# Windowed attention and a gated MLP on one core: softmax sums of four heads in one step, products in 32-column strips, layer norm on three engines, and a new order of all steps

## The chip, the core and the metric

The kernel runs on one core of a Trainium2 chip. The core has a tensor engine (PE; its weight loads are listed apart as PEld), a vector engine (DVE), a scalar engine (ACT), a general engine (POOL) and a sync engine (SP), which issues nearly all DMAs here. Each engine works through its own list of instructions in order, and semaphores hold an instruction back until what it needs is there. Matrix products write to PSUM, of which the kernel uses eight banks of 128 partitions by 512 floats. The metric is the time of one execution on the device in microseconds; lower is better.

## What is computed

Eight batches of eight heads, 576 positions, 64 values per head. First attention over a causal window of 64 positions, then a gated MLP over each position's 512 values, with a layer norm and a product along the positions in it:

```python
scores = scale * np.matmul(q, k.transpose(0, 1, 3, 2))
mask = (rel >= 0) & (rel < window)                 # window = 64
attn = softmax(np.where(mask, scores, -1e9))
x = np.matmul(attn, v)                             # heads side by side: (8, 576, 512)
h = np.maximum(x @ w_in, 0.0)                      # w_in 512 x 1024
u, v = h[..., :512], h[..., 512:]
v_n = (v - mu) / np.sqrt(var + 1e-06)
v_s = np.einsum('ts,bsd->btd', w_spatial, v_n) + b_spatial[None, :, None]
out = (u * v_s) @ w_out                            # (8, 576, 512), float32
```

## The kernel before

Everything is written as named steps, and a step belongs to one engine. `kernel` builds the steps; the text `ORDER` (lines 18 to 145) lists every one of them with its engine and its buffers or PSUM banks, and the instructions are emitted in just that order. So the order of the work on every engine, that of the loads on SP included, is written out by hand. `BUFS` says how many buffers of each kind there are.

The steps, with b for the batch, g for a group of four heads (0 or 1), u for a pair of heads in it:

- `ldq`, `ldk`, `ldv` load a group's inputs (V in five parts); `cq`, `ck`, `cv` cast them to 16 bits on ACT, POOL or DVE (line 292, 295, 298 or 300 in the profile); `tq`, `tk` transpose q and k on DVE (L419); `sl`, `su`, `s4` make `hs`, a copy of V shifted by 64 positions.
- `S` (L479) computes the scores of a group: for seven chunks of keys, four heads and two halves of the head's values, 56 matmuls with 32 rows each, the four heads in four row strips of the array, into two pairs of banks. `E` (ACT, L486) takes the exponential, `M` (DVE, L489) masks it by a minimum.
- `Z` (L502) sums over keys with a matrix of ones: one step for each pair of heads, two matmuls with 64 weight columns over 512 columns. `N` (L529) and `n` (L531) on ACT turn the sums into their inverses by a logarithm and an exponential. `P` (L514) multiplies with V: 14 matmuls for a pair of heads, 64 weight columns each. `X` (DVE, L522) multiplies the two.
- The names ending in `_r` do the same for the last 64 positions of a batch; for batches 4 and 5, and 6 and 7, two batches share these steps (L553 to L606).
- `V` and `U` multiply x with the two halves of w_in, five steps each for a batch; `Vr` (ACT, L670) and `Ur` (ACT, L764) apply the maximum with zero. `Vb`, `Va` (DVE, L672, L674) take mean and variance, `L1`, `L2` (ACT, L717, L719) make the inverse deviation, and `A` (DVE, L729) normalizes, five steps for a batch.
- `G` multiplies with w_spatial along the positions, `Ge` (DVE, L798, L801) multiplies by u, `O` multiplies with w_out, `Oe` (ACT, L647) copies the result out of PSUM, and `st` stores it.
- `D` are warm-up matmuls on zeros (L844), `W` transposes of w_spatial (L378), `ldwin`, `cwin`, `ldwsp`, `cwsp`, `ldwo`, `cwo`, `We` and so on load and prepare the weights.

`V`, `U`, `G` and `O` steps have four or five matmuls of 128 weight columns over 512 columns. In `ORDER` such a step is marked PE, or PH; with PH, `halves` (line 612) issues each matmul as two of 64 weight columns, in the same strips of the array as `Z` and `P`. The fifth step of each (`U_4`, `G_4`) has the last 64 positions: 16 or 20 matmuls over 64 columns (128 where two batches share `U_4`).

Of the kernel before, what the change touches and what calls it, by code (L numbers as in the profile page):

```python
# [10 lines left out]
AF = mybir.ActivationFunctionType  # L11
ALU = mybir.AluOpType
# [18 lines left out]
sl0_11:DVE su0_11:POOL cwin110:POOL N0_r:ACT:4 cwin111:POOL ck1_1:POOL:2 E1_00:ACT:1 X0_00:DVE:0
cwin101:ACT P0_11:PE:3 ldwin011:DQ ldwsp3:DQ:5 ldwsp2:DQ:7 P0_10:PE:1 X0_01:DVE X0_10:DVE:1 n0_r:ACT
D3:PE:0 cq1_1:POOL:0 X0_11:DVE E1_01:ACT:0 ldwsp1:DQ:6 ldwsp4:DQ:1 ldv1_00:DQ:2 P0_r:PE:2 D19:PE:0
V0_2:PH:1 Vr0_2:ACT:0 M1_00:DVE M1_01:DVE X0_r:DVE:0 ldwsp0:DQ:2 V0_3:PH:0 Vr0_3:ACT:1 tk1_1:DVE:6
cwin000:POOL Z1_00:PE:3 N1_00:ACT:5 ldv1_01:DQ ldv1_02:DQ V0_0:PH:1 Vr0_0:ACT:2 tq1_1:DVE:7
cwin010:DVE Vb0_2:DVE:0 cwin001:POOL Vb0_0:DVE:1 n1_00:ACT V0_4:PE:0 V0_1:PH:2 Vr0_4:ACT:3
Z1_01:PE:3 Vb0_4:DVE:2 N1_01:ACT:1 Vb0_3:DVE:3 S1_1:PE:1:0 cwin011:POOL Va0_4:DVE E1_11:ACT:3
E1_10:ACT:2 Va0_0:DVE M1_11:DVE Vr0_1:ACT:4 Vb0_1:DVE:4 cwsp3:POOL:8 U0_0:PE:1 Ur0_0:ACT:0 U0_4:PH:0
cb:POOL cwsp2:ACT ldv1_03:DQ U0_1:PH:3 Ur0_1:ACT:1 Va0_3:DVE U0_2:PE:2 Va0_1:DVE Va0_2:DVE L10:ACT:0
M1_10:DVE Z1_11:PE:1 S1_r:PE:0:1 Ur0_4:ACT:2 L20:ACT A0_1:DVE:0 ldv1_04:DQ U0_3:PE:3 cwsp1:POOL:0  # L40
cwsp4:DVE A0_4:DVE cwsp0:POOL:1 W1:PE:0 E1_r0:ACT:0 A0_0:DVE:1 E1_r1:ACT M1_r:DVE cv1_00:POOL:2
N1_11:ACT:0 ldk2_0:DQ:3 ldv1_10:DQ:3 Ur0_3:ACT:3 W3:PE:1 ldv1_11:DQ ldq2_0:DQ:4 We1:ACT ldv1_12:DQ
W4:PE:3 ldv1_13:DQ We3:ACT cv1_01:DVE We4:DVE sl1_00:DVE:2 W2:PE:0 ldv1_14:DQ ldk2_1:DQ:5 sl1_01:DVE
Ur0_2:ACT:4 ldwo10:DQ:0 ldq2_1:DQ:6 W0:PE:1 We0:DVE Z1_r:PE:3 su1_00:POOL ldwo00:DQ:7 We2:ACT
su1_01:POOL s41_0:POOL cv1_10:POOL:3 sl1_10:POOL:3 N1_r:ACT:2 A0_3:DVE:2 ldwo11:DQ Z1_10:PE:2
N1_10:ACT:3 A0_2:DVE:3 ldwo01:DQ n1_01:ACT P1_00:PE:0 X1_00:DVE:2 P1_01:PE:1 X1_01:DVE n1_10:ACT
G0_0:PH:3 Ge0_0:DVE:0 ldq3_0:DQ:2 ldv2_00:DQ:0 G0_4:PE:2 G0_3:PE:0 ldk3_0:DQ:1 Ge0_4:DVE:1
ck2_0:ACT:1 tk2_0:DVE:2 su1_10:POOL cq2_0:ACT:3 cv1_11:POOL sl1_11:POOL Ge0_3:DVE:2 G0_2:PE:1
s41_1:ACT tq2_0:DVE:3 su1_11:ACT ldv2_01:DQ ldv2_02:DQ ldv2_03:DQ G0_1:PE:3 P1_10:PE:2 P1_11:PE:0
S2_0:PE:0:1 n1_11:ACT X1_10:DVE:3 X1_11:DVE V1_0:PE:2 Ge0_2:DVE:3 ldv2_10:DQ:1 ldv2_11:DQ ldv2_12:DQ  # L50
ldk3_1:DQ:3 U1_1:PE:0 E2_00:ACT:1 M2_00:DVE Ge0_1:DVE:4 E2_01:ACT:0 M2_01:DVE cwo10:POOL
ck2_1:POOL:2 Ur1_1:ACT:5 V1_1:PE:1 ldv2_13:DQ Vr1_1:ACT:5 tk2_1:DVE:4 ldv2_14:DQ ldv2_04:DQ
Vr1_0:ACT:6 Vb1_0:DVE:5 n1_r:ACT V1_2:PE:3 ldv3_10:DQ:2 ldq3_1:DQ:4 P1_r:PE:0 cq2_1:POOL:0 cwo01:ACT
Vr1_2:ACT:7 U1_2:PE:1 cwo00:POOL X1_r:DVE:1 Vb1_1:DVE:2 Va1_0:DVE Ur1_2:ACT:0 cwo11:POOL ldv3_11:DQ
V1_3:PE:2 Vr1_3:ACT:4 Z2_00:PE:0 tq2_1:DVE:5 Vb1_2:DVE:1 N2_00:ACT:4 Va1_1:DVE Z2_01:PE:3
N2_01:ACT:5 V1_4:PE:1 Vr1_4:ACT:3 cq3_0:POOL:1 Oe0_4:ACT:0 U1_3:PH:2 Va1_2:DVE tq3_0:DVE:6
ck3_0:POOL:3 Vb1_4:DVE:3 Vb1_3:DVE:4 S2_1:PE:0:1 E2_10:ACT:2 M2_10:DVE Va1_3:DVE O0_0:PE:0 Va1_4:DVE
tk3_0:DVE:7 E2_11:ACT:3 M2_11:DVE Oe0_0:ACT:0 O0_1:PE:3 Oe0_1:ACT L11:ACT:1 L21:ACT A1_1:DVE:4
A1_0:DVE:5 A1_3:DVE:6 A1_2:DVE:7 A1_4:DVE Ur1_3:ACT:2 cv2_00:POOL:1 sl2_00:POOL:0 su2_00:POOL
O0_2:PE:1 S2_r:PE:0:1 U1_4:PH:0 E2_r0:ACT:0 E2_r1:ACT M2_r:DVE ldv3_12:DQ ldq4_0:DQ:5 ldv3_13:DQ  # L60
cv2_10:POOL:0 U1_0:PH:3 Ur1_0:ACT:3 Z2_10:PE:2 ldv5_10:DQ:3 S3_0:PE:0:1 Ur1_4:ACT:4 Z2_11:PE:3
Oe0_2:ACT:1 n2_00:ACT n2_01:ACT N2_11:ACT:1 G1_3:PH:0 Ge1_3:DVE:5 s42_0:ACT sl2_10:POOL:1 G1_0:PH:1
Ge1_0:DVE:6 ldv3_00:DQ:0 s42_1:ACT su2_10:POOL Z2_r:PE:0 N2_r:ACT:3 N2_10:ACT:0 ldq4_1:DQ:6
ldk4_0:DQ:7 O0_3:PH:3 Oe0_3:ACT st0_1:DQ P2_00:PE:1 X2_00:DVE:0 G1_4:PH:0 Ge1_4:DVE:7 n2_10:ACT
P2_01:PE:2 X2_01:DVE n2_11:ACT ldv4_00:DQ:1 P2_10:PE:3 X2_10:DVE:1 P2_11:PE:1 n2_r:ACT G1_1:PH:0
X2_11:DVE cq3_1:ACT:2 P2_r:PE:2 X2_r:DVE:0 E3_00:ACT:1 ck3_1:POOL:0 U2_0:PE:3 V2_1:PE:1 Vr2_1:ACT:2
Ur2_0:ACT:1 tq3_1:DVE:0 V2_3:PE:2 ldv3_01:DQ ldv3_02:DQ ldv3_03:DQ ldv3_14:DQ cq4_0:POOL:1
Ge1_1:DVE:8 Vr2_3:ACT:1 tk3_1:DVE:1 tq4_0:DVE:8 V2_0:PE:0 U2_4:PE:1 E3_01:ACT:0 M3_01:DVE
Vr2_0:ACT:0 Vb2_0:DVE:0 Ur2_4:ACT:2 st0_4:DQ ldk4_1:DQ:0 cv3_10:POOL:2 Vb2_1:DVE:5 V2_2:PE:3
Vr2_2:ACT:5 st0_0:DQ ldv3_04:DQ S3_1:PE:0:1 E3_10:ACT:2 E3_11:ACT:3 U2_2:PH:2 Ur2_2:ACT:3 G1_2:PH:0  # L70
Vb2_2:DVE:2 Z3_01:PE:1 Vb2_3:DVE:1 N3_01:ACT:2 M3_11:DVE Va2_0:DVE S3_r:PE:0:1 E3_r0:ACT:0 Va2_3:DVE
E3_r1:ACT V2_4:PE:3 Vr2_4:ACT:6 ck4_0:POOL:3 Z3_11:PE:2 N3_11:ACT:4 Ge1_2:DVE:9 O1_2:PH:1
Oe1_2:ACT:1 U2_1:PH:0 Oe1_4:ACT:0 M3_r:DVE Va2_2:DVE Z3_r:PE:2 N3_r:ACT:5 U2_3:PH:1 Vb2_4:DVE:4
M3_10:DVE Va2_4:DVE cq4_1:POOL:2 Va2_1:DVE O1_3:PH:3 L12:ACT:0 L22:ACT M3_00:DVE Z3_10:PE:2
tq4_1:DVE:2 tk4_0:DVE:3 Ur2_3:ACT:4 Ur2_1:ACT:5 A2_0:DVE:0 A2_1:DVE:1 N3_10:ACT:0 Oe1_3:ACT A2_4:DVE
A2_2:DVE:2 A2_3:DVE:3 sl3_10:POOL:2 su3_10:POOL O1_0:PH:1 Z3_00:PE:0 N3_00:ACT:1 s43_1:POOL
ck4_1:POOL:0 cv3_00:POOL:3 sl3_00:POOL:3 s43_0:POOL O1_1:PH:2 ldv4_10:DQ:2 Oe1_0:ACT:0 P3_11:PE:3
ldq5_1:DQ:2 ldq5_0:DQ:1 st1_4:DQ P3_10:PE:0 cq5_1:POOL:1 n3_10:ACT X3_10:DVE:2 ldv5_00:DQ:0
# [821 lines left out]
```

## Time and profile before

| | us |
|---|---|
| three runs | 197.14, 199.26, 199.71 |
| median | 199.26 |
| span of the profiled execution, first to last instruction | 196.2 |
| PE busy, matmuls | 185.6 |
| DVE busy | 161.2 |
| ACT busy | 154.3 |
| POOL busy | 105.5 |

The profiled execution's whole time is not listed beside its span. Busy time is the time in which an engine has at least one instruction running; as matmuls overlap, a busy PE can still be slower or faster than its best. Starts of PE's instructions are therefore of more use than their lengths: the distance from the first matmul of a step to the first of the next is what the step costs.

### The profile page before, as it was taken

Reading aid. Unit: us, or ns where it says so; the run is one execution under the profiler, and the core shown is the slowest. Engines: PE = TensorE matmul, PEld = TensorE weight load, DVE = VectorE, ACT = ScalarE, POOL = GpSimd, SP = SyncE. Lnnn points to the kernel's source line nnn. Section 1 sums busy time; section 2 is a strip of 40 time slices with the busy share of each in tenths; the row PEclk is TensorE's granted clock in tenths of the full one; section 3 lists DMA queues with packets and bytes.
Section 4 is the critical chain, followed back from the end, with each engine's and each line's share of the span. In section 5 each row is a group of like instructions: output and inputs, shape, how many; then the busy total and the mean of one; then the engine's idle time right before and its main releaser. Section 6 shows DMA issues by size and latency. Waiting matters only on the chain.

```text
span 196.2 us, 7598 instructions
## 1 busy us (share of the span) xinstructions
PE 185.6 (95%) x3211; PEld 105.8 (54%) x3211; DVE 161.2 (82%) x297; ACT 154.3 (79%) x275; POOL 105.5 (54%) x188
## 2 busy tenths in 40 slices
PE   7789899899999999999999998999999999999991
PEld 2334545545454655665565655665765565655550
DVE  4699999999998899999999995979985983846440
ACT  2479779995998989997899996888897997736331
POOL 4265684857988549950999965939756000000000
PEclk9999999999999999999999999999999999999999
DMA  6996999999989988698977799496934002400625
GB/s 207 397 294 172 354 358 252 278 336 381 264 207 283 334 225 242 192 253 240 331 201 233 160 267 327 78 295 197 344 120 147 3 3 109 133 7 0 226 74 189
DMA packets 50277, 42.73 MB, mean 218 GB/s; under 512 B 39361, under 2 KB 39489, under 8 KB 50242
## 3 DMA queue, kind: packets, MB, share of 16 engines
q1 hardware_dynamic: 50018, 41.91, 71.8%
q8 instruction: 25, 0.41, 1.0%
q10 hardware_dynamic: 224, 0.33, 0.5%
q14 instruction: 10, 0.08, 0.2%
HBM read 32.79 MB, written 9.44 MB: 215 GB/s over the span
## 4 chain that ended last, share of the span: by engine, by line
PE 70%; DVE 15%; DMA 6%; ACT 4%; issue 2%; POOL 1%; SPq 0%; DVEq 0%; POOLq 0%
PE bank L617 48%; PE bank L614 7%; PE bank L514 4%; PE pair L479 4%; PE bank L703 3%; DMA out_dram<-ob 3%; DMA nk<-in_k_dram 3%; PE bank L502 2%; DVE kT L419 2%; DVE vn L729 2%; ACT e L486 2%; DVE qT L419 2%; DVE e L489 2%; DVE st L672 1%; DVE hv L300 1%
## 5 line engine op out<-in xcount | busy, mean ns | idle before, releaser
L617 PE MATMUL bank<-wspT,vn 128*64 128x512 f16 (+3 forms) x460 | 35.7, 300 | 0.6 <-DVE vn L729 0.6
L486 ACT ACTIVATE e<-pair 128x1024 f16<-128x1024 f32 x32 | 31.6, 1024 | 5.6 <-PE pair L479 4.8
L295 POOL CAST hk<-nk 128x384 f16<-128x384 f32 x42 | 23.4, 593 | 16.8 <-DMA nk<-in_k_dram 16.5
L647 ACT COPY ob<-bank 128x512 f32<-128x512 f32 (+1 forms) x39 | 22.4, 593 | 10.9 <-PE bank L617 7.7
L617 PE MATMUL bank<-x,win 128*64 128x512 f16 (+2 forms) x368 | 30.2, 304 | 0.0
L798 DVE TENSOR_TENSOR g<-bank,ru 128x512 f16<-128x512 f32 (+1 forms) x36 | 22.9, 650 | 7.2 <-PE bank L617 6.7
L617 PE MATMUL bank<-wout,g 128*64 128x512 f16 x232 | 28.5, 379 | 0.0
L672 DVE BATCH_NORM_STATS2 st<-vs 128x6 f32<-128x512 f16 (+1 forms) x40 | 25.8, 668 | 3.0 <-ACT vs L670 2.8
L670 ACT ACTIVATE vs<-bank 128x512 f16<-128x512 f32 (+1 forms) x40 | 23.2, 598 | 5.9 <-PE bank L617 3.1
L298 POOL COPY hs<-hv 64x512 f16<-64x512 f16 (+1 forms) x44 | 26.3, 624 | 1.2
L764 ACT ACTIVATE ru<-bank 128x512 f32<-128x512 f32 (+1 forms) x38 | 21.8, 581 | 5.8 <-PE bank L617 5.5
L489 DVE TENSOR_TENSOR e<-e,mask 128x1024 f16<-128x1024 f16 x32 | 24.0, 762 | 2.6 <-ACT e L486 2.5
L617 PEld LDWEIGHTS <-vn 128*64 128x64 f16 (+1 forms) x460 | 18.3, 110 | 13.6 <-DVE vn L729 2.0
L617 PE MATMUL bank<-win,x 128*64 128x512 f16 x192 | 24.3, 379 | 0.0
L522 DVE TENSOR_TENSOR x<-bank,lz 128x512 f16<-128x512 f32 x32 | 20.9, 681 | 3.9 <-PE bank L514 3.8
L295 POOL CAST hq<-nq 128x384 f16<-128x384 f32 x33 | 17.3, 560 | 10.4 <-DMA nq<-in_q_dram 10.3
L419 DVE STREAM_TRANSPOSE qT<-hq 128x576 f32<-128x576 f32 x16 | 19.8, 1240 | 2.6 <-ACT hq L292 2.5
L419 DVE STREAM_TRANSPOSE kT<-hk 128x576 f32<-128x576 f32 x16 | 19.7, 1239 | 0.5 <-POOL hk L295 0.5
L617 PEld LDWEIGHTS <-win 128*64 128x64 f16 x368 | 15.1, 111 | 9.3 <-issue 0.8
L529 ACT ACTIVATE lz<-bank 128x512 f32<-128x512 f32 x32 | 19.1, 603 | 0.8 <-PE bank L502 0.8
L531 ACT ACTIVATE lz<-lz 128x512 f32<-128x512 f32 x32 | 19.5, 631 | 0.3
L729 DVE TENSOR_SCALAR vn<-vs,mv,ln 128x512 f16<-128x512 f16 (+1 forms) x40 | 17.7, 492 | 2.3 <-ACT ln L719 2.3
(89 smaller groups left out, 294.1 us busy)
## 6 DMA issues: line engine op xcount, KB each, us to landing
nq<-in_q_dram SPq DMA_DIRECT2D x16, 576.0 KB, 6.6
nk<-in_k_dram SPq DMA_DIRECT2D x16, 576.0 KB, 5.5
nv<-in_v_dram SPq DMA_DIRECT2D x64, 128.0 KB, 5.2
out_dram<-ob SPq DMA_DIRECT2D x14, 512.0 KB, 5.5
wi<-in_moe_w_in_dram SPq DMA_DIRECT2D x8, 256.0 KB, 5.6
ws<-in_moe_w_spatial_dram SPq DMA_DIRECT2D x4, 288.0 KB, 7.3
nv<-in_v_dram SPq DMA_DIRECT2D x16, 64.0 KB, 4.9
wo<-in_moe_w_out_dram SPq DMA_DIRECT2D x4, 256.0 KB, 7.2
```

What stands on the lines that cost most here:

```text
L295: nc.gpsimd.tensor_copy(o[:, n:n + 384], i[:, n:n + 384])
L298: nc.gpsimd.tensor_copy(o[:, lo:hi, :, :], i[:, lo:hi, :, :])
L419: d = add(f"t{name}{b}_{g}", ("DVE", 1.09), key, lambda e: nc.vector.transpose(qt.t[:, :].rearrange("p (i j) -> p j i", j=18), h.t[:, :].b ...
L486: ex = add(f"E{b}_{g}{u}", ("ACT", 0.91), key, lambda e, u=u: nc.scalar.activation(e2[u].t[:, :, :], sc[u].t[:, :, :], AF.Exp, bias=0.0, s ...
L489: mins.append(add(f"M{b}_{g}{u}", ("DVE", 0.65), key, lambda e, u=u: nc.vector.tensor_tensor(e2[u].t[:, :, :], e2[u].t[:, :, :], mask[:, : ...
L617: nc.tensor.matmul(o[c:c + 64, :], w[:, c:c + 64], x, start=start, stop=stop)
L647: lambda e: (nc.vector.tensor_copy if last else nc.scalar.copy)(view(), m.t[rows, 0:n]),
L670: rl = add(f"Vr{b}_{j}", ("ACT", 0.49), key, lambda e: nc.scalar.activation(vs.t[0:jn, :], m.t[0:jn, :], AF.Relu), deps=[pv], acq=[vs], us ...
L672: s1 = add(f"Vb{b}_{j}", ("DVE", 0.6), key + 0.02, lambda e: nc.vector.bn_stats(st6.t[0:jn, 0:6], vs.t[0:jn, :]), deps=[rl], acq=[st6], us ...
L729: ENG[e].tensor_scalar(o[0:jn, :], VS[j].t[0:jn, :], mv_t[b % NSB][0:jn, j, 0:1], ln.t[0:jn, 5 + j:6 + j], ALU.subtract, ALU.mult)
L764: lambda e, m=m, ru=ru, n=n: nc.scalar.activation(ru.t[:, 0:n], m.t[:, 0:n], AF.Relu), deps=[pu], acq=[ru], uses=[m])))
L798: nc.vector.tensor_tensor(g.t[:, 0:n], m.t[:, 0:n], ru.t[:, 0:n], ALU.mult)
```

## The change

1. `Z` has one step for a group of four heads: four matmuls of 32 weight columns over 512 columns, one bank, and with it one `N` and one `n` in place of two each. `Z_r` likewise, over half the columns.
2. `P` still has two steps for a group, but a step now holds all four heads and every second of a head's 64 values (`f::2`): 28 matmuls of 32 weight columns, where 14 of 64 were. `P_r` doubles its matmuls likewise. x then holds its 512 values in another order, and the rows of w_in are loaded in that order.
3. The helper `halves` becomes `strips`, with a third form PQ: 32 weight columns, four matmuls where one was. In the new `ORDER`, 133 of the `V`, `U`, `G`, `O` steps are PQ, 18 are PE, none is PH (before: 115 PH and 36 PE). `V_4` takes its strips by the same helper.
4. `A` may run on DVE, POOL or ACT: 19, 10 and 11 of the 40 (before: 40 on DVE). On ACT it needs a bias, mean times inverse deviation, negative; a new step `B` makes it after `L2`, four on DVE and four on POOL. The `A` on DVE and POOL wait for `L2`, those on ACT for `B`.
5. The casts and copies `cq`, `ck`, `cv`, `sl`, `su`, `s4` may run on DVE for every batch, not the first two alone.
6. `ORDER` is another one throughout: engines, buffers, banks, the places of the warm-up steps (D12 and D21 now stand between the `O` steps of batch 0), and the order of the loads on SP.

```diff
@@ FORMS
-HALVED = {w.split(":")[0] for w in ORDER.split() if w.split(":")[1] == "PH"}
+FORMS = {"PE": 128, "PH": 64, "PQ": 32}
+WIDTH = {w.split(":")[0]: FORMS[w.split(":")[1]] for w in ORDER.split() if w.split(":")[1] in FORMS}
@@ Z and P of a group
-        for u in (0, 1):
-            zb, ob = buf("bank", f"z{b}_{g}{u}"), buf("bank", f"o{b}_{g}{u}")
...
-                    for w in (0, 1):
-                        nc.tensor.matmul(zb.t[64 * w:64 * w + 64, :], ones[:, :], e2[u].t[:, w, :],
-                                         start=True, stop=True)
+        zb, lz = buf("bank", f"z{b}_{g}"), buf("lz", f"lz{b}_{g}")
...
+                for hh in range(4):
+                    nc.tensor.matmul(zb.t[32 * hh:32 * hh + 32, :], ones[:, 0:32],
+                                     e2[hh // 2].t[:, hh % 2, :], start=True, stop=True)
...
-                        for w in (0, 1):
-                            nc.tensor.matmul(ob.t[64 * w:64 * w + 64, qs],
-                                             vv[:, (c + 1) // 2, 2 * u + w, :],
-                                             e2[u].t[:, w, qs],
+                        for hh in range(4):
+                            nc.tensor.matmul(ob.t[32 * hh:32 * hh + 32, qs],
+                                             vv[:, (c + 1) // 2, hh, f::2],
+                                             e2[hh // 2].t[:, hh % 2, qs],
                                              start=True, stop=True)
@@ strips
-    def halves(name, o, w, x, start, stop):
-        if name not in HALVED:
-            nc.tensor.matmul(o[:, :], w, x, start=start, stop=stop)
-            return
-        for c in (0, 64):
-            nc.tensor.matmul(o[c:c + 64, :], w[:, c:c + 64], x, start=start, stop=stop)
+    def strips(name, o, w, x, start, stop):
+        wd = WIDTH[name]
+        for c in range(0, w.shape[1], wd):
+            nc.tensor.matmul(o[c:c + wd, :], w[:, c:c + wd], x, start=start, stop=stop)
@@ layer norm
+        def emit_B(e, ln):
+            if e == "DVE":
+                nc.vector.scalar_tensor_tensor(ln.t[:, 10:15], mv_t[b % NSB][:, :, 0], -1.0,
+                                               ln.t[:, 5:10], ALU.mult, ALU.mult)
+                return
+            nc.gpsimd.tensor_scalar(ln.t[:, 10:15], mv_t[b % NSB][:, :, 0], -1.0, None, ALU.mult)
+            nc.gpsimd.tensor_tensor(ln.t[:, 10:15], ln.t[:, 10:15], ln.t[:, 5:10], ALU.mult)
...
             def emit_A(e, j=j, jn=jn, vn=vn):
                 o = vn.t if vn is not None else vn4_t[b % NSB]
+                if e == "ACT":
+                    nc.scalar.activation(o[0:jn, :], VS[j].t[0:jn, :], AF.Identity,
+                                         bias=ln.t[0:jn, 10 + j:11 + j], scale=ln.t[0:jn, 5 + j:6 + j])
+                    return
@@ rows of w_in
-                                 st.t[:, 512 * f:512 * f + 512], moe_w_in[256 * g + 128 * f:256 * g + 128 * f + 128, cs]),
+                                 st.t[:, 512 * f:512 * f + 512], rows[:, f, :]),
```

The new `ORDER` around three places that the prediction speaks of (batch 0 and 1, the layer norm of batch 3, and that of batch 5):

```
O0_0:PE:0 D12:PE:3 O0_2:PE:1 Ur1_0:ACT:1 cq3_0:POOL:3 Va1_4:DVE O0_1:PE:2 D21:PE:3 tk3_0:DVE:6
L11:ACT:1 ldv2_13:DQ ldq3_1:DQ:2 Oe0_0:ACT:0 L21:ACT E2_10:ACT:1 B1:DVE M2_01:DVE O0_3:PE:0 A1_4:DVE
A1_1:POOL:4 A1_0:POOL:5 ldv2_04:DQ ldv3_10:DQ:2 tq3_0:DVE:7 A1_3:DVE:6 ldv2_14:DQ ldk4_0:DQ:7
...
ck5_0:POOL:3 cq5_1:POOL:1 ... L13:ACT:1 ... L23:ACT ... B3:POOL ck5_1:POOL:2 ... A3_2:DVE:4 ... A3_4:DVE
... S5_0:PE:0:1 U3_0:PE:0 Oe2_3:ACT A3_0:ACT:5 A3_1:ACT:6 A3_3:ACT:7 ... E5_01:ACT:2 Ur3_0:ACT:5
E5_00:ACT:3 ... G3_2:PE:3
...
cv7_10:POOL:2 ... L15:ACT:1 L25:ACT ... B5:POOL A5_4:POOL A5_3:POOL:4 ... cv7_00:POOL:3 ... A5_1:POOL:7
```

348 lines of the change are left out of this document (172 added, 176 removed).

## The prediction

> **What bounds the kernel now.** I read the page first (parts 1, 2 and 4), then busy time by stages, then the tensor engine's (PE's) instructions in order of time.
>
> ```profile
> span 196.2 us, 7598 instructions
> ...
> PE 185.6 (95%) x3211; PEld 105.8 (54%) x3211; DVE 161.2 (82%) x297; ACT 154.3 (79%) x275; POOL 105.5 (54%) x188
> ...
> PEclk9999999999999999999999999999999999999999
> ...
> PE 70%; DVE 15%; DMA 6%; ACT 4%; issue 2%; POOL 1%; SPq 0%; DVEq 0%; POOLq 0%
> ```
>
> The clock is full throughout, and the chain that ended last is mostly PE. Busy time alone proves little, since matmuls overlap, so the stages decide; each row gives its bounds, its length, then the busy time of PE, weight loads, DVE, ACT and POOL.
>
> ```profile
> 0.00:24.50 24.50, 20.08 (x330) 9.66 (x330) 19.43 (x36) 15.79 (x24) 12.68 (x29) 1.00 0.90 285
> 24.50:39.40 14.90, 14.08 (x223) 7.64 (x224) 14.15 (x30) 13.59 (x28) 10.74 (x17) 1.00 1.06 296
> 39.40:192.00 152.60, 151.41 (x2672) 88.48 (x2665) 127.18 (x232) 124.78 (x225) 82.13 (x144) 1.00 0.68 201
> ```
>
> Stage A ends where V0_2, the first product with w_in, starts; stage B where G0_0 starts; stage C with PE's last matmul. In C, PE is without work for 1.2 of 152.6 us, while DVE and ACT have some 25 us free. Whether PE works at its own pace there is seen in its timeline (start, length, instruction):
>
> ```profile
> 97.75 1.03 PE L617 MATMUL bank<-x,win 128*64 128x512 f16 x8
> 98.61 0.38 PE L502 MATMUL bank<-e,ones 128*64 128x512 f16 x2
> 98.83 1.03 PE L617 MATMUL bank<-wout,g 128*64 128x512 f16 x8
> 99.79 0.67 PE L479 MATMUL pair<-qT,kT 32*128 32x128 f16 x56
> 100.39 0.25 PE L514 MATMUL bank<-e,hv 128*64 128x128 f16 x2
> ...
> 100.66 0.67 PE L617 MATMUL bank<-x,win 128*64 128x64 f16 x32
> 101.16 1.25 PE L617 MATMUL bank<-wspT,vn 128*64 128x512 f16 x10
> ```
>
> Distances between starts are what counts. A U step (eight half-width matmuls, 97.75 to 98.61) takes 0.86: 0.216 for each pair of 64-column strips over 512 columns, or 0.42 ns a column. The two strips of a pair therefore run beside each other. Z (98.61 to 98.83) takes one such 0.216. The O step before the scores takes 0.96 and not 0.86, so a change of strip shape costs 0.10. S takes 0.60 for 56 matmuls; one after the other, 56 matmuls over 4096 columns would take 1.7 us, so its four row strips run four abreast. Everything in C is priced by such distances, and only what shortens PE's list, or removes one of its few waits, shortens C.
>
> **The change, part by part.**
>
> Z. In 32-column strips one Z step serves four heads: four matmuls of 512 columns in place of two steps with two. If four column strips run abreast, a step stays at 0.216 and every second one goes. In C there are 24 of them (batches 2 to 7): 12 x 0.216 = 2.6 us gone. The remainder's Z_r works over half the columns: in C two of 0.11 (two pairs over 128 columns at 0.42 ns) and two of 0.22, halved, 0.3 gone. The trace has two column strips and four row strips abreast, never four column strips; the ends are 2.9 us saved and nothing saved. I take 2.9, because S shows that four strips can be fed at once. [...]
>
> P. It now has 28 matmuls of 32 weight columns where it had 14 of 64.
>
> ```profile
> 82.12 0.49 PE bank L514 x28
> ```
>
> That row of the chain is two P steps: 0.245 each for 512 columns, 17.5 ns for a matmul with its weight load. Four abreast the columns still need 0.21, but there is only half the time for each instruction, 8.75 ns. S spends 0.60, or 0.50 without its change of shape, on 56: 8.9 ns. So 28 take 0.25, and P costs nothing more. The other end is the 17.5 ns of P itself: 0.49 a step. I take 0.245, by S, which is the only row with four strips.
>
> V, U, G, O. 133 of these steps move to four 32-column strips. A group of four over 512 columns stays at 0.216 by the same argument, as there is time for 54 ns an instruction pair. Only steps over 64 columns could come to be bound by instructions; their rows are U3_4 above (32 matmuls, 0.50) and G1_4 below (40, 64.38 to 65.02, 0.64). Twice the number at 8.9 ns gives 0.57 and 0.71; the 32-wide G_4 are six and the single U_4 four, so nought to 0.7 us, and I take nought, as the columns need 0.5 anyway.
>
> ```profile
> 60.17 0.60 PE L617 MATMUL bank<-wspT,vn 128*64 128x512 f16 x4
> 61.18 2.10 PE L617 MATMUL bank<-wspT,vn 128*64 128x512 f16 x16 [0.41 <-DVE vn L729]
> 63.12 0.28 PE L582 MATMUL bank<-er,ones 128*64 128x128 f16 x4
> ...
> 64.38 0.83 PE L617 MATMUL bank<-wspT,vn 128*64 128x64 f16 x40
> 65.02 0.25 PE L514 MATMUL bank<-e,hv 128*64 128x128 f16 x2
> ```
>
> Changes of shape. With Z, P and most products in one shape, walking both lists from G0_0 on gives 40 changes before and 33 after: 7 x 0.10 = 0.7 gone.
>
> Two warm-up steps, D12 and D21, now stand between the O steps of batch 0, inside C: two matmuls of 512 columns each, 4 x 0.216 = 0.9 added, unless PE would wait there.
>
> So C's list of PE shrinks by 2.6 + 0.3 + 0.7 - 0.9 = 2.7.
>
> Other engines.
>
> ```profile
> L529 ACT ACTIVATE lz<-bank 128x512 f32<-128x512 f32 x32 | 19.1, 603 | 0.8 <-PE bank L502 0.8
> L531 ACT ACTIVATE lz<-lz 128x512 f32<-128x512 f32 x32 | 19.5, 631 | 0.3
> L729 DVE TENSOR_SCALAR vn<-vs,mv,ln 128x512 f16<-128x512 f16 (+1 forms) x40 | 17.7, 492 | 2.3 <-ACT ln L719 2.3
> L298 POOL COPY hs<-hv 64x512 f16<-64x512 f16 (+1 forms) x44 | 26.3, 624 | 1.2
> ```
>
> ACT loses 16 logarithms and 16 exponentials, 19.7 us, and gets 11 normalizations A at about 0.6 (by L531, also from and to SBUF), 6.6. DVE loses 21 A at 0.49, 10.3. POOL gets ten A; none of its kind is in the trace, and I take 0.62 to 1.2 each, nearer the lower row of its copies. It gives up some fourteen casts and copies, so no engine's total rises towards PE's. These savings are worth nothing in C by themselves. Their worth is in the waits. G1_3 and G1_0 above (20 halves, 60.17 to 63.12, 2.95 against 2.16) wait 0.8 us for the five A of batch 1, which run one behind the other on DVE. In the new order they are two on DVE, two on POOL and one on ACT: 0.8 gone. By the steps' prices C holds 3.3 us of waits; these rows and the chain behind them show another 1.1:
>
> ```profile
> 119.22 0.35 PE L597 MATMUL bank<-er,hs 128*64 128x64 f16 x10 [0.30 <-POOL hs L300]
> ...
> 120.67 0.25 PE L514 MATMUL bank<-e,hv 128*64 128x128 f16 x2 [0.24 <-ACT ob L647]
> ```
>
> I leave 2.5 us of waits in C, the order being new; bounds 0.8 and 7.
>
> Stage A. The chain runs through DVE, which copies V:
>
> ```profile
> 6.43 1.41 POOL hk L295 x3
> ...
> 14.63 0.73 DVE hv L300
> ...
> 17.43 0.27 DVE hv L300
> ...
> 19.74 0.87 DVE hv L300 x2
> 20.63 0.58 DVE hs L300
> 21.22 0.67 DVE hs L300
> ```
>
> That is 3.1 us. The new order puts these copies on ACT (which has lost two logarithms and two exponentials there, 2.5) and on POOL; DVE keeps one (0.58) and gets two casts of w_in (0.87 as for two here): 1.7 earlier. Against it, POOL now casts q, k and q in a row before S0_1, 1.41 each, where ACT had done two of them and DVE one. I take 1.3 earlier, 23.2; bounds 1.9 earlier, 0.5 later. Stage B: PE's list is 12.4 of 14.9, all three engines are full, and DVE loses two of five A (1.0): 14.0; bounds 12 and 15.5. So G0_0 starts at 37.2.
>
> Tail.
>
> ```profile
> 191.56 0.46 PE bank L828 x8
> 192.09 0.42 DVE ob L647
> ```
>
> The last result is now a full O step, copied by ACT in some 0.6: 0.2 more than 4.2.
>
> Sum: 23.2 + 14.0 + (152.6 - 2.7 - 0.8) + 4.4 = 190.7 us of span. The profiled execution's own time is not listed; the runs (197.14 to 199.71, median 199.26) lie 0.9 to 3.5 above its span. With the median's 3.1: 193.8.
>
> **The rivals.**
>
> Instruction pairs do not get cheaper (slower). Place: P, P_r, G_4 and single U_4, with 896 + 128 + 480 + 256 = 1760 pairs over 64 columns. At the 17.5 ns of P's row, P gains 32 x 0.245 = 7.8, P_r 1.1, G_4 at 16 ns 6 x 0.64 = 3.8, U_4 4 x 0.5 = 2.0: 14.7, and 208.5 in all. Each ns above 7.5 costs 1.8 us; from 10.6 ns the change gains nothing, from 13 it is over 2% slower. For it: no 32-column weight load is in the trace. Against it: S's 8.9 ns. [...] I give it 0.10.
>
> Four column strips run only two abreast: some 510 groups at 0.216 more, 110 us, about 305. Against it, S; 0.02.
>
> The new order waits elsewhere. B3 (the bias for A on ACT) stands on POOL behind the cast cq5_1, which waits for a load:
>
> ```profile
> POOL hq L295 <- DMA nq<-in_q_dram: 10.3, 6, 3.6
> POOL hv L298 <- DMA nv<-in_v_dram: 4.6, 3, 2.5
> ```
>
> Three A of batch 3 on ACT wait for B3, and behind them on ACT queue E5_01 and E5_00, the evictions of S5_0. A1_1 and A1_0 (behind cq3_0) and A5_1 (behind cv7_00) stand alike. Two such waits of 2.5 to 3.6 not covered, some 6 less the cover, give back the 5.4: 199. For it: POOL's casts run just behind their loads. Against: PE has U3_0 and S5_0 to do meanwhile. 0.18.
>
> The relief takes nearly all waits: C keeps 0.8 and B comes to 12.5, 190.7 - 1.7 - 1.5 + 3.1 = 190.6; with the lowest run's 0.9 in place of 3.1, 188.4; about 189.5. 0.10.
>
> **How the numbers follow.** Forecast 0.60, at 193.8, its own range 190.5 to 197. About 2%, or 195.3 and 203.2, is what a measurement of this kernel can tell from no change. Of the forecast's 0.60, 0.48 lies below 195.3; with the last rival faster has 0.58. The waiting order gives 0.16 to same and 0.02 to slower; same has 0.12 + 0.16 = 0.28, slower 0.02 + 0.10 + 0.02 = 0.14. The range takes in the relief's 189 and, upwards, G0_0 as late as before (2.2) and waits at 7 (4.5): 200.5.
>
> **What would show it.** In the changed profile, Z steps 0.22 apart from the next step with four matmuls, groups of four at 0.216, P at 0.25, and C's list near 146.5 plus waits. G0_0 at 37 or sooner confirms the ramp. The forecast is wrong if P takes 0.4 or more, if the matmuls of a group start one after the other, or if PE's idle time before G3_2 or G5 names POOL or ACT.

## The result and the profile after

The changed kernel takes 234.93 us (median of four runs, 234.07 to 235.77) where the kernel before takes 198.35 beside it: a ratio of 1.188, 95% interval 1.179 to 1.197. It is 36.6 us slower; 193.8 was forecast. Ratios here leave out executions of a slower state that a kernel shows now and then, so they can differ a little from the quotient of the medians. The profiled execution took 234.27 us. From its page, the span, the busy time, the granted clock, the DMA queue that brings instructions (packets, MB, share), and the chain that ended last:

```profile
span 232.6 us, 11564 instructions
...
PE 189.7 (82%) x5205; PEld 105.0 (45%) x5205; DVE 159.5 (69%) x289; ACT 150.1 (65%) x260; POOL 108.7 (47%) x175
...
PEclk9999799979999999999999999799999999999797
...
q8 instruction: 40, 0.66, 1.2%
...
PE 66%; issue 14%; POOL 7%; ACT 4%; DMA 3%; DVE 2%; POOLq 1%; SPq 0%
```

PE's share of the span fell from 95% to 82%, the clock is no longer full everywhere, and 14% of the chain is "issue": time in which an engine waited for nothing that the profile shows. Before it was 2%. No other engine has come near PE, so nothing took PE's place as the bound. What grew is PE's own idle time.

Busy time by stages, cut as the prediction cut it (V0_2, G0_0, PE's last matmul):

```profile
0.00:25.10 25.10, 18.10 (x388) 9.02 (x389) 16.90 (x32) 14.55 (x22) 13.60 (x31) 1.00 0.93 278
25.10:40.20 15.10, 15.07 (x338) 7.42 (x336) 13.51 (x29) 11.92 (x22) 8.07 (x11) 0.89 0.91 270
...
40.20:226.90 186.70, 156.53 (x4481) 88.61 (x4480) 129.13 (x230) 123.11 (x217) 87.04 (x133) 0.97 0.57 167
226.90:232.60 5.70, 0.00 (x0) 0.00 (x0) 0.00 (x0) 0.57 (x1) 0.00 (x0) 0.77 0.36 119
```

Stage C, forecast at 149.1, takes 186.7: 38 of the 42 us by which the span was missed are there. In it PE is idle for 30 us (186.70 less 156.53) where it was idle for 1.2. What ended PE's waits (in total, times, longest):

```profile
PE bank L615 <- issue: 12.1, 7, 3.2
PE bank L615 <- POOL vn L740: 7.0, 4, 2.7
PE bank L511 <- issue: 6.4, 4, 2.5
PE pair L476 <- issue: 3.0, 2, 2.2
PE bank L595 <- issue: 2.6, 2, 2.1
```

L615 are the V, U, G and O steps, L511 is P, L476 is S, L595 is P_r. Two causes show: one without a name, the larger, and A on POOL. PE's timeline shows what the nameless one is (start, length, instruction, count; in brackets the idle time before it):

```profile
44.42 3.36 PE L615 MATMUL bank<-wspT,vn 128*32 128x512 f16 x104 [3.16 <-issue]
47.57 0.30 PE L511 MATMUL bank<-e,hv 128*32 128x128 f16 x2
47.59 0.30 PE L615 MATMUL bank<-wspT,vn 128*32 128x64 f16 x4
47.66 0.26 PE L511 MATMUL bank<-e,hs 128*32 128x64 f16 x2
47.69 0.25 PE L615 MATMUL bank<-wspT,vn 65*32 65x64 f16 x2
47.73 0.32 PE L511 MATMUL bank<-e,hv 128*32 128x64 f16 x4
47.78 0.31 PE L511 MATMUL bank<-e,hs 128*32 128x64 f16 x3
47.84 0.24 PE L511 MATMUL bank<-e,hv 128*32 128x64 f16 x1
47.84 0.26 PE L511 MATMUL bank<-e,hs 128*32 128x64 f16 x1
47.91 0.25 PE L511 MATMUL bank<-e,hv 128*32 128x64 f16 x2
47.96 0.25 PE L511 MATMUL bank<-e,hs 128*32 128x64 f16 x2
50.72 0.21 PE L511 MATMUL bank<-e,hv 128*32 128x64 f16 x3 [2.51 <-issue]
```

PE stands idle twice, and both times in the middle of a step whose operands are ready. The first stop is behind 10 of the 20 matmuls of G0_0. The second is inside P1_00: by the L511 rows 17 of its 28 matmuls stand before it, so that of the four matmuls, one for each head, which read the same chunk of `hv` and `e`, one stands before the stop and three (x3) behind it. Counting the x column from the first stop to the second gives 127 matmuls (one either way is the resolution of such a count). Each has its own weight load (the page counts 5205 of both), so some 256 instructions. Numbered from the start of the program, PE's long nameless stops come at these matmuls:

```
matmul  mod 128  inside  at us   us from the start before
   351       95  P0_10   23.62   1.98
   735       95  G0_0    44.42   3.55
   862       94  P1_00   50.72   2.75
  1118       94  U1_4    61.19   2.18
  1502       94  G1_1    81.01   2.48
  1630       94  G1_2    84.84   1.79
  1886       94  U2_4    95.59   1.77
  2142       94  P3_00  104.42   1.76
  2270       94  G2_4   108.15   1.78
  2398       94  S4_1   114.89   2.43
  3293       93  P5_r   147.03   2.25
```

With five shorter ones, at the same remainder, they come to 28.5 us. The instruction queue q8 brings one packet of 16 KB (0.66 MB by 40) for each 128 matmuls: (5205 - 94) / 128 is 39.9, and the page has 40. For the kernel before it is 24.4, and its page has 25:

```profile
q8 instruction: 25, 0.41, 1.0%
```

Each long stop ends 1.2 to 1.6 us after the end of such a packet. The stop at 44.42 follows the packet that lies in this window (41.60 to 42.90, answer of the DMA view):

```profile
q8 instruction: 1, 0.02, 5.7%
```

So the reading was: PE works through blocks of 256 instructions; the next block is fetched while the current one runs, and not a whole block earlier (in this kernel and the one before, the earliest packet began 0.9 and 1.2 us before PE's first matmul of the current block); and where 256 instructions hold less work than the fetch takes, PE is idle until the next ones are there. Times of the fetches in this trace and in three of the experiments below give what it takes: a packet begins 1.0 us (median of 59) after PE entered the block before it where the DMA engines were mostly idle, 2.6 us (median of 47) where they were full; it lasts about 1.0; PE goes on 1.4 later. That makes 3.4 to 5.0 us. With one middle value of 4.2 for all blocks, chosen after the fact, the stops of this kernel come out at 26 to 28 us, by how a block's undisturbed length is read, and those of the kernel before at none: its shortest block lasted 4.5 us. This is an estimate with a fitted value; the experiments test it.

### The profile page after: what moved, and what is told of

The parts are those of the page before. It is cut to its first block, busy times and chain, and to the rows that moved or that the text cites. A ratio compares the mean times of both kernels' runs of the same rounds, so it can differ in the third digit from the quotient of the medians.

```text
span 232.6 us, 11564 instructions
## 1 busy us (share of the span) xinstructions
PE 189.7 (82%) x5205; PEld 105.0 (45%) x5205; DVE 159.5 (69%) x289; ACT 150.1 (65%) x260; POOL 108.7 (47%) x175
## 2 busy tenths in 40 slices
DMA packets 50292, 42.97 MB, mean 185 GB/s; under 512 B 39361, under 2 KB 39489, under 8 KB 50242
## 4 chain that ended last, share of the span: by engine, by line
PE 66%; issue 14%; POOL 7%; ACT 4%; DMA 3%; DVE 2%; POOLq 1%; SPq 0%
PE bank L615 53%; POOL vn L740 5%; PE bank L511 4%; PE pair L476 3%; DMA nk<-in_k_dram 3%; PE bank L854 2%; PE bank L497 2%; DVE qT L416 1%; POOLq L511 1%; PE bank L375 1%; ACT vn L737 1%; PE bank L595 1%; ACT e L483 1%; ACT ob L645 1%; PE pair L550 1%
## 5 line engine op out<-in xcount | busy, mean ns | idle before, releaser
L615 PE MATMUL bank<-wspT,vn 128*32 128x512 f16 (+6 forms) x1100 | 48.5, 305 | 15.4 <-issue 8.2
L615 PE MATMUL bank<-win,x 128*32 128x512 f16 (+1 forms) x552 | 42.7, 402 | 0.1
L615 PE MATMUL bank<-x,win 128*32 128x512 f16 (+4 forms) x800 | 37.6, 304 | 3.9 <-issue 3.9
L615 PEld LDWEIGHTS <-vn 128*32 128x32 f16 (+3 forms) x1100 | 24.0, 99 | 35.8 <-issue 12.1
L809 DVE TENSOR_TENSOR g<-bank,ru 128x512 f16<-128x512 f32 (+1 forms) x36 | 23.2, 654 | 24.2 <-PE bank L615 22.7
L615 PE MATMUL bank<-wout,g 128*32 128x512 f16 (+2 forms) x524 | 39.4, 377 | 0.0
L740 POOL TENSOR_SCALAR vn<-vs,mv,ln 128x512 f16<-128x512 f16 (+1 forms) x10 | 23.4, 2344 | 21.3 <-ACT ln L725 12.2
L615 PEld LDWEIGHTS <-x 128*32 128x32 f16 (+1 forms) x552 | 18.4, 101 | 18.2 <-issue 5.2
L615 PEld LDWEIGHTS <-win 128*32 128x32 f16 (+1 forms) x800 | 18.3, 96 | 17.7 <-issue 5.8
L486 DVE TENSOR_TENSOR e<-e,mask 128x1024 f16<-128x1024 f16 x32 | 23.8, 760 | 0.4 <-ACT e L483 0.4
L294 POOL COPY hs<-hv 64x512 f16<-64x512 f16 (+1 forms) x30 | 17.4, 612 | 13.9 <-DVE hv L296 13.2
L615 PEld LDWEIGHTS <-g 128*32 128x32 f16 (+1 forms) x524 | 17.3, 97 | 10.7 <-DVE g L809 0.2
```

Source lines behind the costliest of these rows:

```text
L486: mins.append(add(f"M{b}_{g}{u}", ("DVE", 0.65), key, lambda e, u=u: nc.vector.tensor_tensor(e2[u].t[:, :, :], e2[u].t[:, :, :], mask[:, : ...
L615: nc.tensor.matmul(o[c:c + wd, :], w[:, c:c + wd], x, start=start, stop=stop)
L740: ENG[e].tensor_scalar(o[0:jn, :], VS[j].t[0:jn, :], mv_t[b % NSB][0:jn, j, 0:1], ln.t[0:jn, 5 + j:6 + j], ALU.subtract, ALU.mult)
L809: nc.vector.tensor_tensor(g.t[:, 0:n], m.t[:, 0:n], ru.t[:, 0:n], ALU.mult)
```

## The experiments

The kernel before ran beside every experiment (medians 197.3 to 198.4 us), the changed kernel did not; differences from its 234.93 us therefore carry about 1 us.

**Full width again.** All V, U, G and O steps in 32-column strips go back to full-width matmuls; Z and P stay in four strips. The first words of `ORDER` that change:

```diff
-V0_2:PE:3 V0_3:PQ:2 V0_4:PQ:0 V0_0:PQ:1
+V0_2:PE:3 V0_3:PE:2 V0_4:PH:0 V0_0:PE:1
...
```

> The changed kernel with its V, U, G and O steps (those in four 32-column strips) back to full-width matmuls of 128 columns; V_4 and the last O, whose weights have 64 columns, take two strips of 64. Z and P stay in 32-column strips, order, engines and loads stay as they are. Theory one, supply of instructions (PE takes its instructions in blocks of 256, and a block cannot be used up in less than about 4.2 us): the program falls from 5205 to about 3100 matmuls, q8 from 40 packets to about 24, PE's stalls named 'issue' from 28.7 us to about 6; changes of strip shape rise by about 69 x 0.10 = 6.7, so 15 to 19 us less than the changed kernel, 215 to 220. Rival, the normalizations on POOL and the new order are what costs: PE's waits stay and only the changes of shape are added, about 241. Rival, strips in themselves are slow: the steps' start-to-start prices of 0.216 a group should fall visibly below 0.216; theory one has them unchanged.

Measured: 218.2 us (217.46 to 219.19), 1.105 times before (1.095 to 1.114). From its page and PE's waits:

```profile
q8 instruction: 24, 0.39, 0.8%
```

```profile
PE bank L615 <- POOL vn L740: 6.7, 3, 2.9
PE bank L511 <- issue: 6.1, 3, 4.1
...
PE bank L615 <- issue: 1.6, 1, 1.6
```

The nameless waits fall, those for A on POOL stay, and although about 69 more changes of strip shape cost some 6.7 us (an estimate, at the 0.10 us that one took in the kernel before), the time falls by 16.7 us, inside the 15 to 19 expected. PE's four stops of this kind now sum to 8.5 us, not 6: the first one alone is 4.3. So 20 of the 28.5 us went with the 32-column strips of V, U, G and O; 8.5 stay in a program that still has P's doubled matmuls and the new order.

**Moving the block ends.** One warm-up step gets 40 more matmuls, in time in which PE waits for its first operands. After it the program is the same.

```diff
-            for c in range(2 if i < NWARM - NFILL else FILL):
-                n = 512 if i < NWARM - NFILL else 128
+            for c in range(42 if i == 1 else 2 if i < NWARM - NFILL else FILL):
+                n = 64 if i == 1 else 512 if i < NWARM - NFILL else 128
```

> The changed kernel with 40 matmuls more in its second warm-up step: 42 of 64 columns in place of two of 512, in time in which PE waits for its first operands; everything after it is the same instruction for instruction. Theory one (blocks of 256 PE instructions, one matmul and its weight load being two): all block ends move 40 matmuls earlier in the program, so the stalls named 'issue' move too: from a matmul index of 94 in each 128 to the same index counted with the 40 new ones, which is 54 of 128 in the old count. By lengths of the blocks without stalls and a floor of 4.2 us the long stalls come at S1_0, V1_2, V1_4, P2_01, S4_0, G2_4, V4_3, S6_0, G4_0, G5_4 and the sum falls from 27.9 to about 22.6, so about 5 us less, 229. Rival, a cause in the order (a dependency, a semaphore, an engine that is late): the stalls stay at the steps where they are, and the time stays within 1 us of 234.9.

Measured: 230.84 us (229.24 to 233.34). The stops over 1 us with the releaser "issue", in the profiled execution:

```
matmul  mod 128  inside  at us   us from the start before
   863       95  G0_4    46.23   2.68
   990       94  V1_2    52.80   3.48
  1246       94  V1_4    66.47   2.92
  1502       94  P2_01   82.59   1.69
  1630       94  P2_11   86.16   1.33
  2142       94  S4_0   106.01   3.13
  2398       94  S4_1   117.03   2.73
  3165       93  V4_3   145.68   2.30
```

The remainder is the same and the steps are others: five of the ten places named beforehand have a stop of over 1 us, and where the kernel stood before (P1_00, G1_1, P3_00, G2_4, P5_r) it now runs through. The stops sum to 22.3 us (22.6 expected), the time is 4.1 less (5 expected). A dependency would have stayed at its step. This settles that the stops belong to places in the instruction stream.

**Only the number of instructions, in the kernel before.** The V, U, G and O matmuls in strips are cut into pieces of 128 columns (a second kernel: 256); strips, order, engines and loads are untouched.

```diff
         for c in (0, 64):
-            nc.tensor.matmul(o[c:c + 64, :], w[:, c:c + 64], x, start=start, stop=stop)
+        n = x.shape[1]
+        wd = 128 if n == 512 else n
+        for a in range(0, n, wd):
+            for c in (0, 64):
+                nc.tensor.matmul(o[c:c + 64, a:a + wd], w[:, c:c + 64], x[:, a:a + wd],
+                                 start=start and a == 0, stop=stop and a + wd == n)
```

> The kernel before with every 512-column matmul of its V, U, G and O steps in 64-column strips cut into four of 128 columns: the same work, the same strips, the same order, engines and loads, only 5887 matmuls in place of 3211. Theory one (supply of instructions): walking the blocks of 128 matmuls through the old kernel's own times, 22 blocks lie in less than 3.5 us and 33 in less than 4.2, together 10 us short of the one and 30 of the other; so PE gets stalls named 'issue' at a matmul index of 94 in each 128, q8 goes from 25 packets to about 46, and the time rises by 10 to 30 us, some 20: 208 to 228. Rival, 32-column strips, the new order or the normalizations are the cause: nothing of them is in this kernel, the time stays within 3 us of 198.2. Rival, each matmul costs more by itself: the groups would start further apart than 0.216 us, evenly, and not at one place of the block.

> As the run that cuts into four, with cuts into two of 256 columns: 4103 matmuls. Theory one: only four blocks lie in less than 4.2 us, two of them in less than 3.5, together 0.9 to 3.0 us short; the time rises by 1 to 3 us, 199 to 201.5, with stalls at G1_3, G3_0, O3_0 and O5_0. A cost per matmul would give a third of what the cut into four gives, 3 to 10 us.

Measured: cut into four, 230.38 us (226.40 to 231.76), 1.156 times before (1.140 to 1.172); cut into two, 202.70 (201.59 to 205.31), 1.026 (1.016 to 1.037); before, 197.29. The cut into four, from its page, its waits and PE's timeline:

```profile
q8 instruction: 45, 0.74, 1.3%
```

```profile
PE bank L620 <- issue: 16.8, 14, 2.6
PE pair L479 <- issue: 3.9, 3, 2.9
```

```profile
161.07 0.23 PE L479 MATMUL pair<-qT,kT 32*128 32x128 f16 x1
164.25 0.66 PE L479 MATMUL pair<-qT,kT 32*128 32x128 f16 x55 [2.95 <-issue]
```

Here L620 are the cut matmuls. S7_0 stands for 2.95 us after the first of its 56 matmuls. All fifteen nameless stops over 0.6 us have a remainder of 94 or 95 by 128, and they sum to 23.8 us. So the cause needs neither 32-column strips, nor the new order, nor the new normalizations: more instructions for the same work suffice. Part of the excess is what the second rival said: a U step goes from 0.864 to 0.894 us, 0.03 for each of 105 steps, 3 us. Stops and this together are 27 of the 29 us by which the profiled execution (226.40) lies above the kernel before. The cut into two lies above what was expected. It has 1.1 us of that kind, one stop of 2.3 at none of the four places named (its packet began 4.1 us after PE had entered the block before), and behind it a stretch at half clock (0.988 over the run).

**A on DVE.** The ten normalizations go from POOL to DVE at the same places of the order.

```diff
-A1_1:POOL:4 A1_0:POOL:5
+A1_1:DVE:4 A1_0:DVE:5
...
```

> The changed kernel with its ten normalizations A from POOL put on DVE, at the same places of the order. Theory one (instruction supply is the large cost, A on POOL the second): PE's waits for A on POOL (3.1 before G1_3, 0.9 before G4, 1.9 and 2.7 before G5_0 and G7_0) go, and with them perhaps one window of half clock, 7 to 10 us less: 225 to 228; the stalls named 'issue' stay within 2 us of 28.7, at the same matmuls. Rival, POOL's normalizations and what queues behind them are the main cost: 30 us or more less, 205 or below.

Measured: 229.54 us (227.78 to 230.79), 5.4 less than the changed kernel. A's instructions in the changed kernel (count, busy time, mean ns), then in this one (min, median, max ns):

```profile
L740 POOL TENSOR_SCALAR vn<-vs,mv,ln 128x512 f16<-128x512 f16 (+1 forms) x10 | 23.4, 2344 | 21.3 <-ACT ln L725 12.2
```

```profile
L740 DVE TENSOR_SCALAR vn<-vs,mv,ln x29: 317/401/751, 42.1 to 210.2; 128x512 f16<-128x512 f16 x23, 64x512 f16<-64x512 f16 x6
```

One A takes 2.34 us on POOL and 0.40 on DVE. PE's waits for it are gone, and the rival, that POOL is the main cost, falls with 30 us not seen. The gain is below the 7 to 10 expected: the first stop grew from 2.0 to 3.9 us, and three more windows of half clock fell into the kernel (granted clock 0.943 in place of 0.965); on the other side the nameless stops sum to 24.8, outside the 2 us that were allowed.

**Both repairs.** Full width and A on DVE together (one word of each kind):

```diff
-V0_3:PQ:2
+V0_3:PE:2
...
-A1_1:POOL:4
+A1_1:DVE:4
...
```

> The changed kernel with V, U, G and O in full width and the ten normalizations A on DVE in place of POOL, both at once. Theory: the two costs are separate, so the 218.2 us of the full-width kernel lose the 5 to 8 us that POOL's normalizations cost: 210 to 213. What is left above the kernel before is then the 62 added changes of strip shape (about 6) and the stall of the first blocks (4). If supply and normalizations hid each other, it stays above 216.

Measured: 212.69 us (208.88 to 214.98), 1.066 times before (1.052 to 1.080). The two costs add up: 5.5 us from the 218.2 of full width, 5.4 from the changed kernel, though the four runs of this kernel alone spread over 6 us.

**Fewer instructions for U_4 and G_4 alone.** These steps have up to 80 matmuls in 0.65 us.

```diff
-G0_4:PQ:1
+G0_4:PE:1
...
```

> The changed kernel with only its U_4 and G_4 steps (64 columns, up to 80 matmuls in 0.65 us) back to full width: 4605 matmuls in place of 5205, 18 more changes of strip shape (1.7 us). Theory: the blocks' floor of 4.2 us leaves 12.4 us of stalls in place of 27.9, so 10 to 14 us less than the changed kernel: 221 to 225. If only the number of matmuls counted, and not how short the work of a block is, 600 of the 2000 extra ones would be worth 30% of 28.7 less 1.7, some 7 us: 228.

Measured: 223.03 us (221.92 to 229.58), 11.9 less than the changed kernel; stops of 13.7 us in place of 28.5. Taking away 30% of the added matmuls takes away half of the stops; the number alone would have given 7 us. That the shortness of their blocks makes the difference is likely and not shown by this run alone: the block ends now fall at other steps too, and moving them alone had changed the stops by 6.2 us (28.5 to 22.3).

**Data traffic.** First fewer packets: V's loads in rows of 1 KB.

```diff
-    nv.t[0:sn, c, :, :],
-    v[b, 4 * g:4 * g + 4, 128 * c:128 * c + sn, :].transpose([1, 0, 2])),
+    nv.t[0:sn, c, :, :].rearrange("p h d -> p (h d)"),
+    v[b, 4 * g:4 * g + 4, :, :].rearrange("h (p x) d -> (h p) (x d)", x=4)[128 * c:128 * c + sn, :]),
```

> The changed kernel with V's loads read in rows of 1 KB in place of rows of 256 bytes: the same bytes and the same number of loads, a quarter of the packets; V's elements then lie at other places, so the output is not the reference's. It asks why the fetch of a block begins 1.2 to 3.3 us after the one before was used up early in the run, and 0.3 to 1.3 us after it late. Theory one with a crowded DMA queue: the early delays fall towards 0.3 to 1.3, the stalls from 28.7 to 15 to 22 us, and the time by 6 to 13 us. Theory one without it (the delay has another cause): stalls and time stay within 3 us of the changed kernel's, apart from waits for V itself.

Measured: 232.2 us (229.41 to 237.97), 2.7 less, with stops of 26.1 us in the profiled execution (237.97). With 22,644 packets in place of 50,292 the time stays within the 3 us of the second theory, far from the 6 to 13 of the first, so the number of packets is not what mainly delays a fetch. Then more bytes: loads that nobody reads, in the changed kernel and, as a control, in the one before.

```diff
+    MORE = {"ldv7_04": 7, "st4_4": 9, "st5_0": 9}
+    count = [0]
...
+        for _ in range(MORE.get(s.name, 0)):
+            d = pool.tile([128, 1152], f32, tag=f"nat_{count[0] % 6}", bufs=1, name=f"more{count[0]}")
+            nc.sync.dma_start(d[:, :], q[count[0] % 8, 0:4, :, :].rearrange("h (i j) d -> (h i) (j d)", j=18))
+            count[0] += 1
```

> The changed kernel with 25 more loads of 0.59 MB each behind its last ones, into buffers of q and k that are free by then; nobody reads them. They fill the DMA engines from about 166 to 215 us, where the changed kernel leaves them mostly idle. It asks whether data traffic lengthens the fetch of a block of instructions: in the four profiles so far the fetch begins 1.0 us (median) after PE has begun the block before where DMA is idle, and 2.6 us where it is full. Theory: blocks in this stretch, of which seven last less than 5 us, now stall PE; 5 to 9 us more than the changed kernel, 240 to 244, with new stalls named 'issue' between 166 and 215 us. Rival, what delays the early fetches is something other than traffic: no new stalls there, within 2 us of 234.9.

> The control: the kernel before with 18 such loads behind its last ones (from about 148 to 184 us). Its blocks last 4.5 to 11 us there. Theory: at most one or two short stalls, 0 to 2 us more than 197.3 to 198.2. Rival, loads of themselves slow the other engines or the stores: 4 us or more.

Measured: 242.98 us (242.00 to 243.93), 8.1 more than the changed kernel; the control 196.91 (195.28 to 200.94), 0.995 of before (0.990 to 0.999). Stretches with the loads (the last three columns are the granted clock, the share of DMA, and GB/s): the changed kernel without them, the changed kernel with them, the control.

```profile
165.00:215.00 50.00, 46.66 (x1352) 26.09 (x1336) 33.72 (x68) 35.45 (x63) 19.58 (x24) 1.00 0.22 71
```

```profile
165.00:215.00 50.00, 41.95 (x1244) 22.95 (x1236) 30.69 (x58) 31.85 (x55) 17.17 (x23) 0.97 0.73 261
```

```profile
148.00:184.00 36.00, 36.00 (x568) 20.81 (x566) 22.73 (x50) 25.62 (x47) 2.13 (x5) 1.00 0.95 357
```

With DMA at 0.73 PE loses 4.7 us more in this stretch than with 0.22, and the stops at block ends there go from 0.8 to 9.4 us; at one of them, matmul 4445, from 0.79 to 4.07. In the control PE is busy without a gap at a DMA share of 0.95: in the kernel before, the blocks of this stretch last 4.5 to 10.7 us, while seven blocks of the changed kernel's stretch last 2.6 to 4.7 even without the loads. The packets show what the traffic does. For the five blocks that PE entered between 173 and 195 us with the loads, the packet began 1.7 to 3.8 us after the entry, and 0.2 to 1.2 us after it for the same blocks without; the packet itself took 0.9 to 1.3 us in both. So in these runs a busy DMA delayed the start of the fetch, and cost PE time only in the kernel with the short blocks. Why the start waits is open.

**A mix.** Each V, U, G and O step in the form that leaves no block much shorter than 4.2 us with few changes of shape, A on DVE. The lines have the same form as those of the two repairs, with PE or PQ chosen for each step.

> The changed kernel with its V, U, G and O steps in full width or in 32-column strips, each as chosen so that no block of 256 instructions is much shorter than 4.2 us and few changes of shape are added (3829 matmuls, 92 changes from V0_2 on where the changed kernel has 41 and the one before 48), and A on DVE. Theory: PE's list from V0_2 on is 163.3 us against 161.6 of the kernel before and 158.4 of the changed one, stalls 3.5 in place of 27.9, plus the 4 of the first blocks: 202 to 208. So no mix beats the kernel before, since what the summing in four strips takes off the list, changes of shape and fetches give back. Rival, the waits that the change was to remove are worth several us: below 198.

Measured: 208.45 us (207.49 to 209.41), 1.056 times before (1.048 to 1.064), just above what was expected; three stops of 4.7, 2.5 and 1.4 us are left. No form of the changed kernel that was run beats the kernel before.

## Why the prediction was wrong

The sum was 190.7 us of span, the span is 232.6. By its own terms:

Stage A, 23.2 forecast, 25.1: the fetch stop inside P0_10 (1.98) is as large as the difference. Stage B, 14.0 forecast, 15.1: a window at half clock lies in it (0.89 over the stage).

PE's list in C was right. With the prices of the prediction it is 146.5, and the steps of the changed kernel, where nothing interrupts them, cost just that:

```profile
19.53 0.23 PE bank L511 x28
...
168.11 0.23 PE bank L497 x4
168.33 1.76 PE bank L615 x32
```

In these rows of the chain that ended last a P step with its 28 matmuls takes 0.23, a Z step with four strips 0.22 (168.11 to 168.33), two U steps 1.76. So four column strips ran abreast here, and in the P step a matmul with its weight load followed the one before it after 8.2 ns (0.23 by 28). The first two rivals, dearer instruction pairs and strips two abreast, fall. The list did become 2.7 us shorter, as forecast.

The step that failed is **"V, U, G, O. 133 of these steps move to four 32-column strips"**, costed at nought "as there is time for 54 ns an instruction pair". That priced an instruction by whether PE can start it in time. It did not ask how 62% more of them reach PE. The working has no row of q8; the page had one, and its 25 packets for 3211 matmuls would have given blocks of 128 and, for 5205, blocks of 4.7 us on average in a span of 190, with P, S and the 64-column steps far below that. In C the steps with a stop at a block's end take 26.5 us more than their prices. None of the prediction's rivals had this cause; its slower rivals had a chance of 0.14 together, for other reasons.

The second is **"Other engines"**: A on POOL taken at 0.62 to 1.2 us, "nearer the lower row of its copies". It takes 2.34. "No engine's total rises towards PE's" was true and beside the point, since PE waits for single A's: before G1_3, G4_3, G5_0 and G7_0, 7.8 us in C. The prediction's own sign for error, PE's idle time before G3_2 or G5 naming POOL or ACT, appeared: at G5_0 with POOL (1.5 us), at G3_2, much smaller, with ACT (0.1 us). The rival "The new order waits elsewhere" named A1_1, A1_0 and A5_1 too, but for another reason: casts on POOL that wait for loads. A1_1 and A1_0, before G1_3, begin after 9.14 us in which POOL is idle, and then take 5.82 together:

```profile
68.47 5.82 POOL L740 TENSOR_SCALAR vn<-vs,mv,ln 128x512 f16<-128x512 f16 x2 [9.14 <-DMA nv<-in_v_dram]
```

The row names a load of V, which A does not read; no such load lands between 65.28 and 69.10. What ended just before 68.47 is L2 of batch 1 on ACT (68.15 to 68.36), which A needs, and cq3_0 was done 9 us earlier. So it is not a late load but the length of two A, one behind the other. Before G4_3 and G7_0 two A on POOL stand one behind the other in the same way (4.67 and 4.45 us together). A5_1, before G5_0, stands behind two A and the cast cv7_00, with no idle time between them. So the order has a part there; late loads have none in these four waits. B3, the rival's first place, began 8.1 us after POOL's cast cq5_1 had ended, held up by nothing but batch 3's means.

The third is a term that was missing, the clock, taken as full because it was full before. After some stops of PE it fell to half for windows of 3.41 us (length, PE's busy time, and at the end clock, DMA share and GB/s):

```profile
44.42:45.65 1.23, 1.23 (x24) 0.66 (x28) 0.36 (x1) 0.40 (x1) 0.00 (x0) 1.00 1.03 280
45.65:49.06 3.41, 2.56 (x111) 1.83 (x100) 1.45 (x3) 0.00 (x0) 1.33 (x3) 0.50 1.03 391
```

This one begins 1.2 us after the stop before 44.42 ended. There are three in C; in them the steps that hold no stop take 4.4 us more than their prices. In the 3.41 us just before these windows PE is idle for 2.19, 2.05 and 2.32 us, and in no other such stretch of C for more than 1.89; two of them hold a fetch stop, the third the wait for A on POOL before G7_0. The window in stage B began after a stretch with 1.79 us of idle time, less than that 1.89. So that the idle time brings the half clock is a reading of these places; no run was made for it.

What is left in C, 1.5 us, stands against the 2.5 of waits that were allowed. 146.5 + 26.5 + 7.8 + 4.4 + 1.5 is 186.7. The tail takes 5.7 and not 4.4: ACT issues one of the last stores for 2.3 us (226.89 to 229.20) before it can issue the other. Why is not shown.

What it costs PE to go from one block to the next differs between the two kernels. In the kernel before, where the shortest block lasted 4.5 us, no stop falls on a block's end; in the changed kernel such a stop takes up to 3.55 us (before 44.42), and by the estimate above it would be hidden only from a block of 3.4 to 5.0 us on.

## What to carry to other kernels

Count PE's instructions before splitting matmuls into strips or pieces: besides its columns, each 256 instructions needed several microseconds of work here (by the estimate above, 3.4 with mostly idle DMA, 5.0 with full), and a single dense stretch counted, not the average. The waits named "issue" that came at even distances in the instruction count, at 93 to 95 by 128, were the instruction supply here; 40 cheap matmuls put in early moved them to other steps at the same remainder, which no dependency would do. A step handed to an idle engine is to be priced on that engine by its own kind of instruction (A on POOL took 2.34 us where its copies take 0.62), and by who waits for the single one, not by the engine's total.

## What the hardware showed unexpectedly

The fetch did not run ahead by more than a block: no packet of the two kernels began more than 1.2 us before PE's first matmul of the current block. A long block gave the one after the next no credit: G0_0 stood still until 44.42 although PE had taken 7.3 us over the block before last. Data traffic entered by how full the DMA engines were and not by the number of packets: 22,644 packets in place of 50,292 left the stops nearly as they were (26.1 us, 28.5 before), and filling the DMA engines (a share of 0.73 in place of 0.22) raised one stop from 0.79 to 4.07 us.

A tensor_scalar with two operations over 512 columns took 2.34 us on POOL (mean; 2.06 to 3.25) and 0.40 on DVE (median), a factor of 5.8, while POOL's copies of half the partitions, which had served as the estimate, take 0.62.

In four windows of 3.41 us the granted clock was 0.50 while PE still had work. They begin at 25.17, 45.65, 148.05 and 216.32 us, that is 6, 30 and 20 times 3.41 us apart. PE was not idle throughout the 3.41 us ahead of the second: of those before 45.65 it was idle for 2.19 and had worked again for the last 1.2. A stop that lies across two such stretches left the clock as it was and one inside a stretch did not: the 2.69 us before 74.34 did, the 2.06 before 147.03 did not.
